# A one-token gated decode kernel: the order of the last weight loads, and the engine that sums w2

## The chip, the cores and the metric

The kernel runs on one core of a Trainium2 chip. Its engines are named as in the profile: TensorE (PE, matrix products; PEld is its weight load), VectorE (DVE), ScalarE (ACT), GpSimd (POOL) and SyncE (SP, which here only issues transfers). The metric is device time in microseconds. Three runs of the kernel before gave 693.84 to 693.93 us, with a median of 693.9 us.

## The reference

One token x (512 values) goes through two branches that a gate mixes. Everything is float32.

```python
x = A_x
g = _sigmoid((x * gate_w).sum(-1, keepdims=True))
a = _A_ref(x, A_k_cache, A_v_cache, A_wq, A_wo)   # attention
b = _B_ref(x, B_w1, B_w3, B_w2)                   # (silu(x w1) * (x w3)) w2
return g * a + (1 - g) * b
```

The attention has 32 query heads and 8 key/value heads of 128, with 32,768 positions in the cache: q = x wq, a softmax over q k / sqrt(128), the weighted sum of v, and then a product of all 4,096 head outputs with wo (4096 x 512). The other branch has 1,792 hidden values, and w2 is 1792 x 512. The key cache and the value cache are 128 MiB each; wo and wq are 8 MiB each, w1, w3 and w2 3.5 MiB each.

## The kernel before

The two caches are read once, each in 16 units of 8 MiB, through two buffers, `big_a` and `big_b`, and a third, `pool_w`, of 4 MiB. All of these loads are issued by SP, in the order in which the program names them; the helper `load` (L190) also makes a load wait until the load nine places earlier has landed, and each load waits until the readers of its buffer are done.

`Program` (L24) is a small scheduler: each operation names what it reads and writes, every engine gets its operations in the order in which the program text names them, and waits are set from these names. So the order of the text is the order of each engine's queue.

The main loop (from L491) goes over the 16 units of keys. A unit is transposed on DVE (L346), multiplied with the query on PE (L330), and every four units the scores are turned and pass a softmax. The units of values follow four steps behind: unit s is half e = s % 2 of head h = s // 2. `values_all` (L426) multiplies it with the weights, and `own` (L442) picks each head's own columns out of the product: a multiply by a mask into `tmp`, and, after a head's second half, a sum over eight blocks into `red[h]`. w1 and w3 come in the middle of the loop, and `hidden` leaves the second branch's hidden values, already times 1 - g, in `htp`: partition p and column k hold hidden value 14 p + k. The last four units of values (12 to 15, heads 6 and 7) come after the loop, and with them all that the change touches:

- `norm` (L533) sums the softmax's denominators over the partitions and takes their reciprocals times the gate.
- `heads` (L541) turns `red[h]` into columns on PE and scales them into `on`: 4 query heads for each key/value head.
- `place` (L553) brings these columns into the layout in which wo's rows lie on the partitions: a multiply on DVE, a product with `spot` on PE, a multiply by a mask on DVE and a sum on DVE.
- `values` (L579) multiplies one half of a unit with the softmax's numerators, 16 products of 128x512, each recorded as two passes.
- `last_head` (L594) does for heads 6 and 7 what `own` and `heads` do for the others, in four operations on DVE, a product and a scaling.
- `mix` (L572) sums 16 rows of wo for each partition on DVE, into `acc`. That is the first half of wo, which waits in `pool_w`; the second half goes through PE.
- `wide` (L656) and `ff_down` (L672) are the last products. `wide` adds products of 32 columns with 128x512 pieces of a weight into the bank `pa`; DVE adds `pa` to `acc`; `ff_down` multiplies the last rows and `acc` (by ones, which sums over the partitions) into the bank `pb`, which is copied out and stored.

The order of the last loads is: unit 12 into `big_a`, the first half of wo into `pool_w`, unit 13 into `big_b`, unit 14 into `big_a`, unit 15 into `big_b` in two halves, the second half of wo and then w2 in five pieces, both into `big_a`. Heads 0 to 5 are laid out (`heads(range(6))` and two calls of `place`) ahead of unit 12's products. Products named `idle_product` (L643) compute nothing that is used.

Of the kernel before, what the change touches and what calls it, by code (L numbers as in the profile page):

```python
# [9 lines left out]
ALU = mybir.AluOpType  # L10
AX = mybir.AxisListType
PE = mybir.EngineType.PE

P = 128
# [102 lines left out]
def kernel(  # L117
# [14 lines left out]
    _, HKV, S, DH = k_cache.shape  # L132
    D = x.shape[-1]
# [27 lines left out]
    def sbuf(name, *shape):  # L161
        return nc.alloc_sbuf_tensor(name, [P, *shape], F32)[:]
# [5 lines left out]
    wo_t = pool_w.rearrange("p (k e) -> p k e", k=16)  # L168
    wo_l = big[0][:, R:2 * R].rearrange("p (k e) -> p k e", k=16)
    sb = sbuf("sb", 16, 32, 4)  # L170
    win = sbuf("win", NP, 4, 48)
# [7 lines left out]
    red = [sbuf(f"red{h}", P) for h in range(6)]  # L179
    acc = sbuf("acc", 512)  # L180
    otp = sbuf("otp", 16, 32)
# [8 lines left out]
    def load(dst, src, writes, over=()):  # L190
        lanes[0] += 1
        lane = f"load{lanes[0] % 9}"
        return pr.add(
            "SP", lambda: nc.sync.dma_start(dst, src), writes=writes, over=[*over, lane], inc=lane, by=16, also=lane,  # L194
        )

    def region(b, z):
        return big[b][:, z * R:(z + 1) * R]
# [8 lines left out]
    own_b, own_q, own_k, own_x = sbuf("own_b", 4), sbuf("own_q", 4), sbuf("own_k", 16), sbuf("own_x", 8)  # L207
    spot, mask, xp = sbuf("spot", 16, 8), sbuf("mask", 16), sbuf("xp", NC, 32)
# [11 lines left out]
    for n, t in (  # L220
        ("win0", win), ("otp", otp), ("mt", mt), ("pvpad", pv[:, 512:528]), ("pad0", prob[0][:, 1024:1040]), ("pad1", prob[1][:, 1024:1040])
    ):
        pool(lambda t=t: G.memset(t, 0.0), writes=[n])

    for src, dst, view, axes in (
        ("ident", "fold", "p (c r) -> p r c", dict(c=4)),
        ("fold", "own_b", "p (b q) -> p b q", dict(b=4)),
        ("fold", "own_q", "p (b q) -> p q b", dict(b=4)),

        ("ident", "own_k", "p (x k) -> p k x", dict(k=16)),  # L230
        ("ident", "own_x", "p (x k) -> p x k", dict(k=16)),
        ("ident", "mask", "p (t x) -> p t x", dict(t=16)),
    ):
        tiles = dict(ident=ident, fold=fold, own_b=own_b, own_q=own_q, own_k=own_k, own_x=own_x, mask=mask)
        s = tiles[src][:, 0:16] if src == "fold" else tiles[src]
        dve(lambda s=s, d=tiles[dst], v=view, a=axes: V.tensor_reduce(d, s.rearrange(v, **a), axis=AX.X, op=ALU.add),
            reads=[src], writes=[dst])
    dve(lambda: V.tensor_copy(spot, own_x.unsqueeze(1).to_broadcast([P, 16, 8])), reads=["own_x"], writes=["spot"])
# [23 lines left out]
    for c in range(NC):  # L262
# [14 lines left out]
    dve(lambda: V.tensor_mul(gpr, rows[0][0:1, :], rows[1][0:1, :]), reads=["row0", "row1"], writes=["tmp1"])  # L277
# [3 lines left out]
    dve(lambda: V.tensor_scalar(gate[:, 1:2], gate[:, 0:1], -1.0, 1.0, op0=ALU.mult, op1=ALU.add),  # L281
        reads=["gate0"], writes=["gate1"])
# [159 lines left out]
    def own(s):  # L442
        h, e = divmod(s, 2)
        dve(lambda: V.tensor_tensor(
            tmp[:, e], ps_o.rearrange("p (b d) -> p b d", b=4), own_b.unsqueeze(2).to_broadcast([P, 4, P]), op=ALU.mult,
        ), reads=["o", "own_b"], writes=[f"tmp{e}"])
        if e == 1:
            dve(lambda: V.tensor_reduce(red[h], tmp.rearrange("p e b d -> p d (e b)"), axis=AX.X, op=ALU.add),  # L448
                reads=["tmp0", "tmp1"], writes=[("red", h)])
# [75 lines left out]
    own_rows = sbuf("own_rows", 16)  # L525
    each = [sbuf(f"each{i}", 16, 8 * n) for i, n in enumerate((2, 1))]


    def load_wo(j, dst, key, over=()):
        load(dst, wo[j * 16 * P:(j + 1) * 16 * P, :].rearrange("(p k) e -> p k e", k=16), [key], over=over)  # L530


# [20 lines left out]
    def place(ws, rows, part, keys, over=()):  # L553
        i, n = 2 - len(ws), 8 * len(ws)
        o, m = 8 * ws[0], 8 * (ws[0] % 2)
        mine = each[i]
        dve(lambda: V.tensor_mul(
            mine, on[:, o:o + n].unsqueeze(1).to_broadcast([P, 16, n]), own_k.unsqueeze(2).to_broadcast([P, 16, n]),
        ), reads=["own_k"] + [("on", 2 * w + u) for w in ws for u in range(2)], writes=[f"each{i}"])
        pe(lambda: T.matmul(  # L560
            pm[i][:, 0:16 * n], spot.rearrange("p t x -> p (t x)"), mine.rearrange("p k t -> p (k t)"),
            start=True, stop=True,
        ), reads=["spot", f"each{i}"], writes=[f"m{i}"])
        dve(lambda: V.tensor_mul(
            mine, pm[i][:, 0:16 * n].rearrange("p (k t) -> p k t", t=n),
            mask[:, m:m + n].unsqueeze(1).to_broadcast([P, 16, n]),
        ), reads=[f"m{i}", "mask"], writes=[f"each{i}"])
        dve(lambda: V.tensor_reduce(rows[part], mine[part], axis=AX.X, op=ALU.add),
            reads=[f"each{i}", *over], writes=keys)


    def mix():  # L572
        for k in range(16):
            dve(lambda k=k: V.scalar_tensor_tensor(
                acc, wo_t[:, k, :], own_rows[:, k:k + 1], acc, op0=ALU.mult, op1=ALU.add,
            ), reads=["wo", "own01", "acc"], writes=["acc"])
# [17 lines left out]
    def last_head(h):  # L594
        r = red[h % 2]
        dve(lambda: V.tensor_scalar(r, ps_o[:, 0:P], own_b[:, 0:1], None, op0=ALU.mult),  # L596
            reads=["o", "own_b"], writes=[("red", h % 2)])
        for b in range(1, 4):
            dve(lambda b=b: V.scalar_tensor_tensor(
                r, ps_o[:, b * P:(b + 1) * P], own_b[:, b:b + 1], r, op0=ALU.mult, op1=ALU.add,  # L600
            ), reads=["o", "own_b", ("red", h % 2)], writes=[("red", h % 2)])
        pe(lambda: T.matmul(pm[1][:, 0:REP], r, own_q, start=True, stop=True), reads=["own_q", ("red", h % 2)], writes=["m1"])
        dve(lambda: V.tensor_mul(on[:, 4 * h:4 * h + 4], pm[1][:, 0:REP], recip[:, 4 * h:4 * h + 4]),
            reads=["m1", ("recip", 3)], writes=[("on", h)])

    def load_unit(b, s):
        load(big[b], vd[s // 2, s % 2], ["AB"[b] + str(z) for z in range(2)])

    full, late = slice(0, P), slice(P // 2, P)
    lay = otp[:, :, 0]  # L610
    load_unit(0, 12)
    load_wo(0, wo_t, "wo", ["kt0"])
    load_unit(1, 13)
    own(11)
    norm(range(4))
    heads(range(6))
    place((0, 1), own_rows, full, ["own01"])
    place((2,), lay, full, ["own2"], ["otp"])
# [11 lines left out]
    load_wo(1, wo_l, "A1")  # L630


    w2t = region(0, 0)[:, 0:FR * D].rearrange("p (k e) -> p k e", k=FR)
    w2d = w2.rearrange("(p k) e -> p k e", k=FR)
# [19 lines left out]
    pa, pb = pf[0], pf[1]  # L654

    def wide(ws, **kw):  # L656
        def go():
            for j, (w, t, first, last) in enumerate(ws):
                r = 32 * (j % 4)
                ins = T.matmul(pa[r:r + 32, :], w, t, start=first, stop=last)  # L660
            return ins
        pe(go, writes=["f0"], **kw)

    wide([(otp[:, k, :], wo_l[:, k, :], k < 4, False) for k in range(16)], reads=["own2", "own3", "otp", "A1"])
    for a, b in parts[:2]:
        wide([(htp[:, k, :], w2t[:, k, :], False, k >= 4) for k in range(a, b)], reads=["htp", ("w2", a)])
# [3 lines left out]
    flat = htp.rearrange("p k a -> p (k a)")  # L670
# [94 lines left out]
```

## Time and profile before

| what | value |
|---|---|
| median of the runs | 693.9 us |
| span of the profiled execution | 692.1 us |
| its own time | not given beside it; the median lies 1.8 us above its span |
| read from memory | 296.23 MB, 428 GB/s over the span |
| busy share of the span | PE 56%, DVE 53%, ACT 19%, POOL 0% |
| mean granted clock of TensorE | 0.802 |

A timeline row gives its start and its duration in microseconds, the engine, the line of the kernel, the operation, what it writes and reads, and how many instructions are merged; in brackets stands the idle time of the engine just before it and what ended it. In a table of stretches, each row gives the busy time of every engine in one stretch, then TensorE's granted clock, the DMA share and GB/s. "us to landing" counts from the issue of a load to the event that its data is there, and holds the time in which it stands in the queue behind earlier loads.

### The profile page before, as it was taken

To read this page: it belongs to the slowest core of one execution; us is meant where nothing else is said; L and a number is where in the kernel's file an instruction comes from. 1 tells how busy PE (TensorE), PEld (TensorE's weight loads), DVE (VectorE), ACT (ScalarE), POOL (GpSimd) and SP (SyncE) were. 2 spreads that over 40 slices of the span, in tenths; PEclk is the share of its full clock that TensorE was granted. 3 is DMA by queue.
4 is the path that set the end of the run, shared out by engine and by line. 5 is a ranking of instruction groups with operands and counts; after the bars stand their busy time and mean duration, and the time that the engine had idled before them with its cause. 6 is when DMAs were issued, how large, how long until landed. Compare 5 with 4: busy or idle time off the path is not lost. (4 is left out here: it accounts for less than half of the span.)

```text
span 692.1 us, 5789 instructions
## 1 busy us (share of the span) xinstructions
PE 388.3 (56%) x2448; PEld 95.3 (14%) x2448; DVE 370.1 (53%) x259; ACT 134.7 (19%) x113; POOL 2.8 (0%) x15
## 2 busy tenths in 40 slices
PE   1537677566473636565564646364563646564457
PEld 0101111201010101201010101101010101211112
DVE  1049998493725637493826537492816547600701
ACT  0143323222303131220303131220303031100000
POOL 1000000000000000000000000000000000000000
PEclk9969999968686966778695779788697879865789
DMA  9999999999999999999999999999999999999996
GB/s 394 444 432 424 428 424 432 449 439 432 424 432 424 443 447 432 428 428 428 432 443 443 428 428 428 428 443 447 432 424 428 428 436 439 421 451 425 422 429 287
DMA packets 6213, 296.35 MB, mean 428 GB/s; under 512 B 694, under 2 KB 698, under 8 KB 1084
## 3 DMA queue, kind: packets, MB, share of 16 engines
q1 hardware_dynamic: 6196, 296.23, 99.1%
q8 instruction: 6, 0.10, 0.1%
q14 instruction: 3, 0.02, 0.0%
q10 hardware_dynamic: 8, 0.01, 0.0%
HBM read 296.23 MB, written 0.00 MB: 428 GB/s over the span
## 5 line engine op out<-in xcount | busy, mean ns | idle before, releaser
L346 DVE STREAM_TRANSPOSE aside<-big_a 128x2048 f32<-128x2048 f32 x41 | 94.4, 2302 | 184.3 <-DMA big_a<-in_A_k_cache_dram 184.3
L330 PE MATMUL ps<-aside,winc 128*32 128x512 f32 x512 | 89.4, 776 | 168.0 <-PEq L703 167.2
L330 PE MATMUL ps<-kt,winc 128*32 128x512 f32 x512 | 89.0, 772 | 49.1 <-PEq L703 49.1
L318 ACT COPY aside<-big_a 128x6144 f32<-128x6144 f32 x14 | 74.4, 5313 | 171.2 <-DMA big_a<-in_A_k_cache_dram 171.2
L432 PE MATMUL ps<-big_b,pv 128*32 128x512 f32 x768 | 94.9, 650 | 17.4 <-PEq L703 17.4
L346 DVE STREAM_TRANSPOSE kt<-aside 128x2048 f32<-128x2048 f32 x32 | 72.7, 2273 | 0.0
L346 DVE STREAM_TRANSPOSE kt<-big_a 128x2048 f32<-128x2048 f32 x28 | 63.5, 2269 | 0.0
L330 PEld LDWEIGHTS ps<-aside,winc 128*32 128x32 f32 x512 | 13.1, 120 | 236.6 <-issue 236.6
L358 ACT COPY sb<-ps 128x512 f32<-128x512 f32 x16 | 17.1, 1071 | 136.5 <-PE ps L330 136.5
L432 PEld LDWEIGHTS ps<-big_b,pv 128*32 128x32 f32 x768 | 27.7, 119 | 85.0 <-issue 85.0
L346 DVE STREAM_TRANSPOSE aside<-aside 128x2048 f32<-128x2048 f32 x16 | 36.3, 2269 | 0.0
L587 PE MATMUL ps<-big_b,probs 128*32 128x512 f32 x128 | 19.1, 756 | 21.1 <-DMA big_b<-in_A_v_cache_dram 21.1
L330 PEld LDWEIGHTS ps<-kt,winc 128*32 128x32 f32 x512 | 13.1, 120 | 125.4 <-issue 125.4
L596 DVE TENSOR_SCALAR red<-ps,own_b 128x128 f32<-128x128 f32 x2 | 0.7, 350 | 52.7 <-PE ps L587 52.7
L324 ACT COPY winc<-win 128x128 f32<-128x128 f32 x32 | 9.8, 307 | 77.9 <-PE ps L330 77.9
L587 PE MATMUL ps<-big_a,probs 128*32 128x512 f32 x128 | 18.1, 730 | 7.6 <-DMA big_a<-in_A_v_cache_dram 7.6
L346 DVE STREAM_TRANSPOSE aside<-big_b 128x2048 f32<-128x2048 f32 x7 | 16.0, 2291 | 11.0 <-DMA big_b<-in_A_k_cache_dram 11.0
L641 PE MATMUL ps<-win,ones 128*128 128x512 f32 (+1 forms) x40 | 21.8, 631 | 0.0
L242 PE MATMUL ps<-acc 128*128 128x512 f32 x34 | 20.0, 670 | 2.5 <-POOL acc L213 1.5
L379 DVE TENSOR_REDUCE mt<-turned 128x8 f32<-128x2048 f32 x4 | 9.2, 2292 | 20.3 <-PE turned L368 20.3
L405 DVE TENSOR_REDUCE sums<-probs 128x8 f32<-128x2048 f32 x4 | 15.3, 3834 | 2.1 <-ACT probs L398 2.1
L268 PE MATMUL turned<-big_a,xp 128*32 128x512 f32 x64 | 8.6, 699 | 12.0 <-DMA big_a<-in_A_wq_dram 12.0
(94 smaller groups left out, 186.9 us busy)
## 6 DMA issues: line engine op xcount, KB each, us to landing
big_b<-in_A_v_cache_dram SPq DMA_DIRECT2D x2, 4096.0 KB, 25.8
big_b<-in_B_w_dram SPq DMA_DIRECT2D x2, 3584.0 KB, 20.8
aside<-in_A_wo_dram SPq DMA_DIRECT2D x1, 4096.0 KB, 29.4
big_a<-in_A_wo_dram SPq DMA_DIRECT2D x1, 4096.0 KB, 20.4
big_a<-in_B_w_dram SPq DMA_DIRECT2D x2, 1024.0 KB, 23.5
big_a<-in_B_w_dram SPq DMA_DIRECT2D x1, 768.0 KB, 26.0
big_a<-in_B_w_dram SPq DMA_DIRECT2D x1, 512.0 KB, 26.7
big_a<-in_B_w_dram SPq DMA_DIRECT2D x1, 256.0 KB, 26.9
```

The costliest lines, as they stand in the source:

```text
L242: return T.matmul(ps_s, acc[:, 0:P], acc, start=True, stop=False, skip_group_check=True)
L268: ins = T.matmul(pf[b][32 * j:32 * j + 32, :], xp[:, c, :], t[:, o:o + REP * DH], start=(c == 0), stop=(c == NC - 1),)
L318: act(lambda: A.copy(spare, src[:, :, 32:128]), reads=[key], writes=["wo"])
L324: lambda: A.copy(winc, win[:, t // 4, :, 16 - 16 * z:48 - 16 * z]),
L330: ins = T.matmul(ps_s[32 * g:32 * g + 32, :], winc[:, c, :], kt[c % 2][:, 512 * g:512 * g + 512], start=False, stop=False, skip_group_chec ...
L346: k = dve(lambda d=dst, s=src: V.transpose(d, s), reads=[key], writes=[f"kt{c % 2}"], credit="keys")
L358: lambda: A.copy(sb[:, :, :, t % 4], ps_s.rearrange("p (n i) -> p n i", i=32)),
L379: dve(lambda: V.tensor_reduce(mt[:, 0:8], turned.rearrange("p (n q) -> p q n", q=8), axis=AX.X, op=ALU.max), reads=banks, writes=["mt"])
L405: dve(lambda: V.tensor_reduce(sums[:, 8 * w:8 * w + 8].rearrange("p (u q) -> p u q", u=2), probs[:, :, 0:1024].rearrange("p u (n q) -> p u ...
L432: ins = T.matmul(ps_o[32 * t:32 * t + 32, :], pv[:, o:o + 32], big[1][:, n * P:(n + 4) * P], start=((z, g) == (0, 0)), stop=((z, g) == (1, ...
L587: ins = T.matmul(ps_o[32 * t:32 * t + 32, :], prob[u][:, o:o + 32], vt[:, n * P:(n + 4) * P], start=((e, z, g) == (0, 0, 0)), stop=((e, z, ...
L641: return T.matmul(bank[:, 0:n], ones, win.rearrange("p w c n -> p (w c n)")[:, 0:n], start=True, stop=True)
```

## The change

It does six things.

1. wo is no longer cut in two. It is loaded whole, last, into `big_a`, with 32 of its rows on each partition (`wo_t`), in six pieces of 16, 7, 3, 3, 2 and 1 rows. `mix` and its load go.
2. w2 goes into `pool_w` in one load, issued behind unit 15, ahead of wo. Its product with `htp` is now 14 operations on DVE that add into `acc`.
3. Unit 15 is one load, not two halves.
4. `place` is called twice, once for each half of the heads, behind head 7; `heads` takes all eight heads at once there. It works on 512 elements of each partition, where it had 256 or 128. `norm` stays where it was.
5. `own_head` takes the place of `last_head`: one multiply of 512 elements and one sum over four blocks. `otp`, now 32 x 32, lies in the buffer `kt1` and is cleared on POOL once the scores are done.
6. The masks of the setup, a multiply for the gate and 1 - g are made on POOL, where DVE made them.

The tail's products change places: `wide` takes the first three pieces of wo (26 rows), `ff_down` the last three (6 rows), with the product with `acc` behind the first of these.

```diff
-    wo_t = pool_w.rearrange("p (k e) -> p k e", k=16)
-    wo_l = big[0][:, R:2 * R].rearrange("p (k e) -> p k e", k=16)
+    wo_t = big[0].rearrange("p (k e) -> p k e", k=32)
+    w2t = pool_w[:, 0:FR * D].rearrange("p (k e) -> p k e", k=FR)
...
-    otp = sbuf("otp", 16, 32)
+    otp = kt[1][:, 0:1024].rearrange("p (k c) -> p k c", c=32)
...
+    def summed(dst, src, key, name, o):
+        half = part4[:, o:o + dst.shape[1] * 2].rearrange("p (r c) -> p r c", c=2)
+        pool(lambda: G.tensor_add(half, src[:, :, 0:2], src[:, :, 2:4]), reads=[key], writes=["half" + name])
+        pool(lambda: G.tensor_add(dst.unsqueeze(2), half[:, :, 0:1], half[:, :, 1:2]), reads=["half" + name], writes=[name])
...
+    summed(fold, ident.rearrange("p (c r) -> p r c", c=4), "ident", "fold", 0)
+    summed(own_b, fold[:, 0:16].rearrange("p (b q) -> p b q", b=4), "fold", "own_b", 64)
+    summed(own_q, fold[:, 0:16].rearrange("p (b q) -> p q b", b=4), "fold", "own_q", 72)
+    banded(own_x, 4, 32, "own_x")
+    banded(mask, 32, 4, "mask")
+    pool(lambda: G.tensor_copy(spot, own_x.unsqueeze(1).to_broadcast([P, 32, 4])), reads=["own_x"], writes=["spot"])
...
-    dve(lambda: V.tensor_mul(gpr, rows[0][0:1, :], rows[1][0:1, :]), reads=["row0", "row1"], writes=["tmp1"])
+    pool(lambda: G.tensor_mul(gpr, rows[0][0:1, :], rows[1][0:1, :]), reads=["row0", "row1"], writes=["tmp1"])
...
+    def place(g):
+        mine, part = each[g], slice(64 * g, 64 * g + 64)
         dve(lambda: V.tensor_mul(
+            mine, on[:, 16 * g:16 * g + 16].unsqueeze(1).to_broadcast([P, 32, 16]), fold.unsqueeze(2).to_broadcast([P, 32, 16]),
+        ), reads=["fold"] + [("on", h) for h in range(4 * g, 4 * g + 4)], writes=[f"each{g}"], over=[("sb", m) for m in range(4)])
         pe(lambda: T.matmul(
+            pm[g], spot.rearrange("p t x -> p (t x)"), mine.rearrange("p k t -> p (k t)"), start=True, stop=True,
+        ), reads=["spot", f"each{g}"], writes=[f"m{g}"])
         dve(lambda: V.tensor_mul(
+            mine[part], pm[g][part].rearrange("p (k t) -> p k t", t=16),
+            mask[part, 16 * g:16 * g + 16].unsqueeze(1).to_broadcast([64, 32, 16]),
+        ), reads=[f"m{g}", "mask"], writes=[f"each{g}"])
+        dve(lambda: V.tensor_reduce(otp[part, :, 0], mine[part], axis=AX.X, op=ALU.add),
+            reads=[f"each{g}", "otp"], writes=[("lay", g)])
...
+    def own_head(h):
+        dve(lambda: V.tensor_tensor(
+            tmp[:, h - 6], ps_o.rearrange("p (b d) -> p b d", b=4), own_b.unsqueeze(2).to_broadcast([P, 4, P]), op=ALU.mult,
+        ), reads=["o", "own_b"], writes=[f"tmp{h - 6}"])
+        dve(lambda: V.tensor_reduce(red[h], tmp[:, h - 6].rearrange("p b d -> p d b"), axis=AX.X, op=ALU.add),
+            reads=[f"tmp{h - 6}"], writes=[("red", h)], over=[("sb", m) for m in range(4)])
...
     load_unit(0, 12)
-    load_wo(0, wo_t, "wo", ["kt0"])
     load_unit(1, 13)
+    pool(lambda: G.memset(otp, 0.0), writes=["otp"], over=["kt1"])
     own(11)
     norm(range(4))
-    heads(range(6))
-    place((0, 1), own_rows, full, ["own01"])
-    place((2,), lay, full, ["own2"], ["otp"])
...
-    last_head(6)
-    for z in range(2):
-        load(region(1, z), vd[7, 1][:, z * R:(z + 1) * R], [f"B{z}"])
-    mix()
+    own_head(6)
+    load_unit(1, 15)
+    load(w2t, w2.rearrange("(p k) e -> p k e", k=FR), ["w2"], over=["wo", "kt0"])
     for z in range(2):
         values(7, 0, z, region(0, z), f"A{z}")
...
-    parts = ((0, 4), (4, 8), (8, 11), (11, 13), (13, 14))
+    wod = wo.rearrange("(p k) e -> p k e", k=32)
+    parts = ((0, 16), (16, 23), (23, 26), (26, 29), (29, 31), (31, 32))
     for a, b in parts:
-        load(w2t[:, a:b, :], w2d[:, a:b, :], [("w2", a)], over=["A0"])
+        load(wo_t[:, a:b, :], wod[:, a:b, :], [("wo", a)], over=["A0", "A1"])
...
-    values(7, 1, 0, region(1, 0), "B0")
-    values(7, 1, 1, region(1, 1), "B1")
-    idle_product(512)
-    last_head(7)
-    idle_product(256)
-    place((3,), lay, late, ["own3"], ["own2"])
+    for z in range(2):
+        values(7, 1, z, region(1, z), f"B{z}")
+    own_head(7)
...
+    heads(range(8))
+    for g in range(2):
+        place(g)
     for _ in range(2):
         idle_product(512)
+    for k in range(FR):
+        dve(lambda k=k: V.scalar_tensor_tensor(
+            acc, w2t[:, k, :], htp[:, k, 0:1], acc, op0=ALU.mult, op1=ALU.add,
+        ), reads=["w2", "htp", "acc"], writes=["acc"])
+    laid = ["otp", ("lay", 0), ("lay", 1)]
+    for i, (a, b) in enumerate(parts[:3]):
+        wide(i, [(otp[:, k, :], wo_t[:, k, :]) for k in range(a, b)], reads=[*laid, ("wo", a)])
     dve(lambda: V.tensor_add(acc, acc, pa), reads=["acc", "f0"], writes=["acc"])
...
-    for a, b in parts[2:]:
-        ff_down([(shifted(k), w2t[:, k, :], k == 8, k == FR - 1) for k in range(a, b)], reads=["htp", ("w2", a)])
-        if a == 8:
+    for a, b in parts[3:]:
+        ff_down([(shifted(k), wo_t[:, k, :], k == 26, k == 31) for k in range(a, b)], reads=[*laid, ("wo", a)])
+        if a == 26:
             ff_down([((ones[:, 0:32],) * 2, acc, False, False)], reads=["ones", "acc"])
```

More of the change, by code (lines that the diff above doesn't have):

```diff
@@ L167 @@
     kt = [pool_w[:, NB * 96:NB * 128], sbuf("kt1", NB * 32)]
-    wo_t = pool_w.rearrange("p (k e) -> p k e", k=16)
-    wo_l = big[0][:, R:2 * R].rearrange("p (k e) -> p k e", k=16)
+    wo_t = big[0].rearrange("p (k e) -> p k e", k=32)
+    w2t = pool_w[:, 0:FR * D].rearrange("p (k e) -> p k e", k=FR)
     sb = sbuf("sb", 16, 32, 4)
+    after = sb.rearrange("p n i m -> p (n i m)")
     win = sbuf("win", NP, 4, 48)
@@ L178 @@
     silu, prod = (tmp[:, i].rearrange("p b d -> p (b d)") for i in range(2))
-    red = [sbuf(f"red{h}", P) for h in range(6)]
+    red = [sbuf(f"red{h}", P) for h in range(6)] + [after[:, P * i:P * i + P] for i in range(2)]
+    each = [after[:, 256 + 512 * i:768 + 512 * i].rearrange("p (k t) -> p k t", t=16) for i in range(2)]
     acc = sbuf("acc", 512)
-    otp = sbuf("otp", 16, 32)
+    otp = kt[1][:, 0:1024].rearrange("p (k c) -> p k c", c=32)
     htp = sbuf("htp", FR, 32)
@@ L206 @@
     ident, ones, fold = sbuf("ident", P), sbuf("ones", P), sbuf("fold", 32)
-    own_b, own_q, own_k, own_x = sbuf("own_b", 4), sbuf("own_q", 4), sbuf("own_k", 16), sbuf("own_x", 8)
-    spot, mask, xp = sbuf("spot", 16, 8), sbuf("mask", 16), sbuf("xp", NC, 32)
+    own_b, own_q, own_x = sbuf("own_b", 4), sbuf("own_q", 4), sbuf("own_x", 4)
+    spot, mask, xp = sbuf("spot", 32, 4), sbuf("mask", 32), sbuf("xp", NC, 32)
     gate, sums, recip, on = sbuf("gate", 2), sbuf("sums", 32), sbuf("recip", 32), sbuf("on", 32)
@@ L220 @@
     for n, t in (
-        ("win0", win), ("otp", otp), ("mt", mt), ("pvpad", pv[:, 512:528]), ("pad0", prob[0][:, 1024:1040]), ("pad1", prob[1][:, 1024:1040])
+        ("win0", win), ("mt", mt), ("pvpad", pv[:, 512:528]), ("pad0", prob[0][:, 1024:1040]), ("pad1", prob[1][:, 1024:1040])
     ):
         pool(lambda t=t: G.memset(t, 0.0), writes=[n])
[L225 to L237, printed above, removed]
@@ L238, with banded @@
-    dve(lambda: V.tensor_copy(spot, own_x.unsqueeze(1).to_broadcast([P, 16, 8])), reads=["own_x"], writes=["spot"])
+    def summed(dst, src, key, name, o):
+        half = part4[:, o:o + dst.shape[1] * 2].rearrange("p (r c) -> p r c", c=2)
+        pool(lambda: G.tensor_add(half, src[:, :, 0:2], src[:, :, 2:4]), reads=[key], writes=["half" + name])
+        pool(lambda: G.tensor_add(dst.unsqueeze(2), half[:, :, 0:1], half[:, :, 1:2]), reads=["half" + name], writes=[name])
+    def banded(dst, n, width, name):
+        shape = [[-width, n]]
+        pool(lambda: G.memset(dst, 1.0), writes=[name + "a"])
+        pool(lambda: G.affine_select(
+            out=dst, in_=dst, compare_op=ALU.is_ge, fill=0.0, base=0, pattern=shape, channel_multiplier=1,
+        ), reads=[name + "a"], writes=[name + "b"])
+        pool(lambda: G.affine_select(
+            out=dst, in_=dst, compare_op=ALU.is_ge, fill=0.0, base=width - 1, pattern=[[width, n]], channel_multiplier=-1,
+        ), reads=[name + "b"], writes=[name])
@@ L280 @@
     act(lambda: A.activation(gate[:, 0:1], pm[0][:, 0:1], AF.Sigmoid), reads=["m0"], writes=["gate0"])
-    dve(lambda: V.tensor_scalar(gate[:, 1:2], gate[:, 0:1], -1.0, 1.0, op0=ALU.mult, op1=ALU.add),
-        reads=["gate0"], writes=["gate1"])
+    pool(lambda: G.tensor_scalar(gate[:, 1:2], gate[:, 0:1], -1.0, 1.0, op0=ALU.mult, op1=ALU.add),
+         reads=["gate0"], writes=["gate1"])
     for b in range(2):
@@ L522 @@
     total(NP - 1)
[L525 to L530, printed above, removed]
     def norm(ws):
@@ L592, in values @@
         pe(go, reads=[key, f"pad{u}", ("prob", u)], writes=["o"])
[L594 to L604, printed above, removed]
+    def own_head(h):
[4 more added lines that the diff above has]
+            reads=[f"tmp{h - 6}"], writes=[("red", h)], over=[("sb", m) for m in range(4)])
     def load_unit(b, s):
         load(big[b], vd[s // 2, s % 2], ["AB"[b] + str(z) for z in range(2)])
-    full, late = slice(0, P), slice(P // 2, P)
-    lay = otp[:, :, 0]
     load_unit(0, 12)
-    load_wo(0, wo_t, "wo", ["kt0"])
     load_unit(1, 13)
+    pool(lambda: G.memset(otp, 0.0), writes=["otp"], over=["kt1"])
     own(11)
     norm(range(4))
-    heads(range(6))
-    place((0, 1), own_rows, full, ["own01"])
-    place((2,), lay, full, ["own2"], ["otp"])
     for z in range(2):
@@ L644, in idle_product, with wide, go @@
         pe(lambda: spend(ps_s, n), reads=["ones"], writes=["s"])
-    values(7, 1, 0, region(1, 0), "B0")
-    values(7, 1, 1, region(1, 1), "B1")
-    idle_product(512)
-    last_head(7)
-    idle_product(256)
-    place((3,), lay, late, ["own3"], ["own2"])
+    for z in range(2):
+        values(7, 1, z, region(1, z), f"B{z}")
+    own_head(7)
+    pa, pb = pf[0], pf[1]
+    wides = [b - a for a, b in parts[:3]]
+    final = {j % 4: (i, j) for i, n in enumerate(wides) for j in range(n)}
+    def wide(i, ws, **kw):
+        def go():
+            for j, (w, t) in enumerate(ws):
+                r = 32 * (j % 4)
+                ins = T.matmul(pa[r:r + 32, :], w, t, start=(i == 0 and j < 4), stop=(final[j % 4] == (i, j)))
+            return ins
+        pe(go, writes=["f0"], **kw)
+    heads(range(8))
+    for g in range(2):
+        place(g)
     for _ in range(2):
         idle_product(512)
[L654 to L666, printed above, removed]
+    for k in range(FR):
[5 more added lines that the diff above has]
+        wide(i, [(otp[:, k, :], wo_t[:, k, :]) for k in range(a, b)], reads=[*laid, ("wo", a)])
     dve(lambda: V.tensor_add(acc, acc, pa), reads=["acc", "f0"], writes=["acc"])
-    flat = htp.rearrange("p k a -> p (k a)")
+    flat = otp.rearrange("p k c -> p (k c)")
     def ff_down(ws, **kw):
```

23 lines of the change are left out of this document (1 added, 22 removed).

## The prediction, on record before the result was known

> **What bounds the kernel now.** I read the page's head and its DMA rows first, then the end of the chain of waits, then the timeline of SP, TensorE (PE) and VectorE (DVE) over the last 100 us.
>
> ```profile
> span 692.1 us, 5789 instructions
> ...
> DMA  9999999999999999999999999999999999999996
> GB/s 394 444 432 424 428 424 432 449 439 432 424 432 424 443 447 432 428 428 428 432 443 443 428 428 428 428 443 447 432 424 428 428 436 439 421 451 425 422 429 287
> ```
>
> The DMA engines are busy in every slice but the last. The kernel is one stream of 296 MB, and its time is the stream's length plus what follows the last landing. The change moves the same bytes, so the question is what hangs behind the last loads.
>
> ```profile
> 661.57 26.71 DMA big_a<-in_B_w_dram
> ...
> 688.32 1.10 PE turned L676 x24
> ...
> 689.44 0.29 DVE winc L688
> ```
>
> Today the last piece of w2 lands, 24 product passes follow, and the copy of the result starts at 689.44. The span ends 2.66 us after that (692.1 - 689.44), and the median of the runs, 693.9, lies 1.8 us above the span. Both stay, so I forecast the start of that copy and add its shift to 693.9.
>
> ```profile
> 617.87 0.33 SPq L194 DMA_DIRECT2D big_a<-in_A_v_cache_dram  x1
> ...
> 631.73 9.75 PE L587 MATMUL ps<-big_b,probs 128*32 128x512 f32 x64 [13.93 <-DMA big_b<-in_A_v_cache_dram]
> ...
> 638.11 3.76 SPq L194 DMA_DIRECT2D big_b<-in_A_v_cache_dram  x2
> ...
> 651.09 8.61 PE L587 MATMUL ps<-big_a,probs 128*32 128x512 f32 x64 [7.59 <-DMA big_a<-in_A_v_cache_dram]
> ...
> 659.77 0.33 SPq L194 DMA_DIRECT2D big_a<-in_A_wo_dram  x1
> ...
> 660.80 3.64 PE L587 MATMUL ps<-big_b,probs 128*32 128x512 f32 x32 [1.11 <-DMA big_b<-in_A_v_cache_dram]
> ...
> 670.51 5.70 PE L587 MATMUL ps<-big_b,probs 128*32 128x512 f32 x32 [6.07 <-DMA big_b<-in_A_v_cache_dram]
> ```
>
> Loads land in the order of their issue, 9.7 us for each 4 MiB (660.80 to 670.51), though issued 10 to 20 us earlier. So a load's landing follows from the bytes ahead of it.
>
> **The loads, moved.** Before, 4 MiB of wo go ahead of the last three v units. After, they go behind. Ahead of the end of the last v unit (unit 15) then lie exactly the bytes that now lie ahead of its first half, so it lands at 660.80 (now 670.51), w2 (3.5 MiB, 8.5 us) at 669.3, the first 16 rows of wo at 679.0, and the last piece where it lands now, about 688.9: its last three pieces have the sizes of today's last three.
>
> Does the stream stay fed? Each v unit's buffer comes free when the products of the unit before last end. With landings 9.7 us earlier: unit 13 lands at 622.0, its products end by 631.8 (9.75), so unit 15 is issued at 631.8, and unit 14 lands at 641.4. That is 9.6 us of cover. wo is issued after unit 14's products, by 651.2, and w2 lands at 669.3. w2 itself stands behind unit 15 in SP's queue, and its buffer is free long before. If a cover of 9.6 us were gone, the price would be the gap. I put the loads at nothing.
>
> **The setup, moved to POOL.**
>
> ```profile
> 3.63 0.16 POOL L223 MEMSET probs<- 128x16 f32 x2
> ...
> 23.01 8.62 PE L268 MATMUL turned<-big_a,xp 128*32 128x512 f32 x64 [12.02 <-DMA big_a<-in_A_wq_dram]
> ...
> 31.56 0.38 PE L279 MATMUL ps<-gsm,ones 1*128 1x1 f32 x2
> ```
>
> POOL's queue is empty at 3.8 us. It gets 14 more small operations in the setup, ahead of the gate's product, whose partner on PE runs at 31.56 behind the products with wq, themselves waiting for a DMA until 23.01. At a whole microsecond each (from the 0.08 us of the row above that is far up) they would end at 18. Cost: nothing, hidden under wq's load. The memset of the new otp waits on POOL for the last score products (about 583) and is wanted first near 677. Nothing again.
>
> **Head 6 and what went before it.** The products of heads 0 to 5 and two placings (601.69 to 608.33 in the trace) leave the path ahead of unit 12's products. That only frees a buffer sooner, under a stream that is never starved: no gain. The 16 products of `mix` on DVE with the first half of wo go too, from a stretch where DVE waits anyway (643.62 to 656.17).
>
> **The chain behind unit 15.** It is new: everything of all eight heads is now laid out here, and the 14 sums with w2 stand behind the layout in DVE's queue.
>
> ```profile
> 593.29 1.12 PE L242 MATMUL ps<-acc 128*128 128x512 f32 x2
> ...
> 599.05 0.68 DVE L444 TENSOR_TENSOR tmp<-ps,own_b 128x512 f32<-128x512 f32 x1
> ...
> 599.76 1.87 DVE L448 TENSOR_REDUCE red<-tmp 128x128 f32<-128x1024 f32 x1
> ...
> 601.69 2.72 PE L546 MATMUL ps<-own_q,red 128*128 128x4 f32 x12 [2.10 <-DVE red L448]
> ...
> 604.44 0.18 DVE L549 TENSOR_TENSOR on<-ps,recip 128x24 f32<-128x24 f32 x1 [2.27 <-PE ps L546]
> ...
> 605.14 1.22 PE L560 MATMUL ps<-each,spot 128*128 128x256 f32 x2 [0.73 <-DVE each L557]
> 606.40 0.42 DVE L564 TENSOR_TENSOR each<-ps,mask 128x256 f32<-128x256 f32 x1 [1.31 <-PE ps L560]
> 606.86 0.42 DVE L568 TENSOR_REDUCE own_rows<-each 128x16 f32<-128x256 f32 x1
> ...
> 607.53 0.80 PE L560 MATMUL ps<-each,spot 128*128 128x128 f32 x2 [1.17 <-DVE each L557]
> ...
> 608.26 9.54 PE L587 MATMUL ps<-big_a,probs 128*32 128x512 f32 x64
> ...
> 643.12 0.39 PE L602 MATMUL ps<-own_q,red 128*128 128x4 f32 x2 [1.64 <-DVE red L599]
> ...
> 643.62 12.55 DVE L574 SCALAR_TENSOR_TENSOR acc<-aside,own_rows,acc 128x512 f32<-128x512 f32 x16
> ```
>
> ```profile
> 676.14 1.13 PE L641 MATMUL ps<-win,ones 128*128 128x512 f32 x2
> ...
> 679.35 0.29 DVE L564 TENSOR_TENSOR each<-ps,mask 128x128 f32<-128x128 f32 x1 [0.58 <-PE ps L560]
> ...
> 686.38 0.69 DVE L667 TENSOR_TENSOR acc<-acc,turned 128x512 f32<-128x512 f32 x1 [6.43 <-PE turned L660]
> 687.10 0.86 PE L676 MATMUL turned<-big_a,htp 128*32 128x128 f32 x24 [0.78 <-DMA big_a<-in_B_w_dram]
> ...
> 687.78 0.40 PE L676 MATMUL turned<-acc,ones 128*32 128x128 f32 x8
> ```
>
> Step by step from 660.80, waits of 0.03 to 0.08 between engines included:
> - Unit 15's 64 product passes in one piece. The samples are 9.54, 9.75, 8.61, and 5.70 + 3.64 for the two halves. I take their mean, 9.3: 670.1.
> - Own columns: multiply 0.68; sum over four, 0.94 (half of the 1.87 for eight), with 0.11 of waits: 671.83.
> - Heads, 16 passes. At half clock 2.72/12 each, 3.6 in all; at full clock one head's two passes take 0.39, of which a second pass adds about 0.13, so about 2.2. With 0.05 ahead: 674.1. The scaling (0.18 and gaps): 674.3.
> - Two placings, one after the other, since the second's first multiply stands behind the first's last sum. Each is a multiply, a 128x512 product, a multiply, a sum, all on 512 elements. 128 elements take 0.29, 256 take 0.42, so 512 take 0.69, as the add of L667 does. The product takes 1.13 at full clock (L641). With 0.16 of waits one placing is 3.36; both end at 681.0.
> - 14 sums with w2, each 12.55/16 = 0.784: 10.98, so 692.0. w2 has been there since 669.3; they wait for nothing but their place in the queue.
> - The add of the bank of wo products, 0.72 with its wait: 692.7. That bank is done well before: 26 rows at 3.64 for 16 from about 682, the last of them landing near 685.5.
> - Behind it in PE's queue stand the product with `acc` (8 passes) and the last three rows of wo (24 passes). Those 32 passes take 1.08 (687.10 to 688.18 today): 693.8. The copy starts at 693.9.
>
> So with TensorE at full clock throughout, the copy starts 4.4 us later than 689.44. wo, landed by 688.9, waits for DVE.
>
> **The clock.** This chain has TensorE working in short bursts, and its granted clock falls after pauses:
>
> ```profile
> 599.00:600.00 1.00, 0.41 (x2) 0.30 (x2) 0.96 (x3) 0.00 (x0) 0.00 (x0) 0.81 0.76 328
> 600.00:601.00 1.00, 0.00 (x0) 0.00 (x0) 1.00 (x1) 0.00 (x0) 0.00 (x0) 0.50 0.77 328
> ...
> 641.00:644.00 3.00, 0.86 (x10) 0.30 (x2) 1.86 (x6) 0.00 (x0) 0.00 (x0) 1.00 1.16 502
> 644.00:645.00 1.00, 0.00 (x0) 0.00 (x0) 0.96 (x2) 0.00 (x0) 0.00 (x0) 0.50 0.61 262
> ```
>
> ```profile
> 602.50:612.00 9.50, 7.60 (x33) 3.82 (x37) 2.23 (x7) 0.00 (x0) 0.00 (x0) 0.50 1.04 448
> ```
>
> The third number from the end is the clock (the last two are the DMA share and GB/s). It fell at about 599.8, 5.4 us after the products that ended at 594.4, and at 644.0, 2.5 us after those that ended at 641.5, in spite of a head's burst at 643.12. So a pause of 2.5 to 5.4 us drops it, short bursts not always helping. After 670.1 the second placing's product comes 8 us after the last dense work, with PE busy about half of that time or less. I take it at half clock. Between 602.5 and 612 the clock was 0.50, and there 128 columns took 0.80 and 256 took 1.22, so 512 would take about 2.08 for 1.13: +0.95; both ends, 0 and 0.95, stay in the range, and so do 0 to 0.95 for the first placing and 0 to 1.4 for the heads (3.6 for 2.2). The last 32 passes come some 4 us after the products with wo have run out; 4 us is about two thirds of the way from 2.5 to 5.4, so I take two thirds of doubling 1.08: +0.7, ends 0 and 1.08. Sum: 4.4 + 0.95 + 0.7 = 6.1 us, and 693.9 + 6.1 = **700.0 us**.
>
> The Trainium skill ("TensorE: Matmul & The Clock Gate", Part 1) states that TensorE goes back to half rate after at least one idle window of about 3.4 us. The trace agrees in kind only: idle stretches of 2.5 and 5.4 us both bracket it. By the rule alone the gaps between the placings (under 2.3 us) cost nothing and the pause before the end costs its 1.08, so the sum would be 5.5 us, 699.4.
>
> **The rivals.**
> - *Full clock all the way*: bursts and the two idle products keep TensorE up. For it: at 643.12 a burst still ran at full clock. Against it: the fall at 644.0. It gives 4.4, with 8.6 instead of 9.3 for unit 15 3.7: 697.6 to 698.3.
> - *Half clock all the way* from the heads: 4.4 + 1.4 + 0.95 + 0.95 + 1.08 = 8.8, or 702.7. For it: at 601.69 the heads ran so, 7 us after the last dense work. Against: here they start 1.7 us after.
> - *The sums are hidden*: the stream still sets the end, about 693.9, or at best some tenths less for fewer small pieces. It decides if the layout is done by 677.2 (688.9 for the last landing, less 10.98 and 0.72), that is if the chain from 660.80 takes 16.4 us and not 20.2. The shortest samples for everything give 19.5, so DVE would have to take the sums between the placings, or the sums would have to take 0.5 us each. w2 is in place at 669.3, which speaks for it; the order of DVE's queue speaks against it.
>
> **How the numbers follow.** The forecast (one placing and part or all of the end at half clock, 5 to 7.5 us) gets 0.5; full clock 0.22; half clock throughout 0.15; hidden sums 0.13. The range leaves out the last and a bit of the third: 697.2 (shortest samples) to 703.0. A measurement here can tell about 0.2%, 1.4 us, from no change. Slower by more takes all but the hidden case: 0.87. Of its 0.13, 0.1 is no change and 0.03 faster.
>
> **What would show it.** In the profile after: unit 15's products start near 660.8 and end near 670; w2 landed before that; 14 operations of 0.78 us back to back on DVE from 681 to 692; TensorE idle for some microseconds ahead of the product with `acc`; the chain of waits ends through DVE and not through a DMA; DMA quiet from 689. I would be wrong if the sums began before 678, if the copy's release were a DMA landing, or if a gap stood in the DMA row before 687.

## The result, and the profile after

The kernel after takes 700.37 us (median of 5 runs, 699.85 to 703.13), the kernel before 693.9 us (median of 5 runs, 693.84 to 694.2). The medians lie 6.5 us apart, 0.9%. The ratio over the runs is 1.0101, with a 95% interval of 1.0089 to 1.0112: slower by about 1%. The five runs after fall into two groups, three at 699.85 to 700.37 and two at 702.22 and 703.13. The profiled execution took 699.88 us with a span of 698.1 us, again 1.8 us apart. Its page:

```profile
span 698.1 us, 5779 instructions
...
DMA  9999999999999999999999999999999999999993
GB/s 410 429 421 424 436 422 457 426 424 447 439 428 428 421 454 436 424 428 432 454 424 428 421 451 439 428 421 428 458 432 421 424 443 451 421 428 424 425 424 149
```

The stream is as full as before up to the last slice, and there it is thinner: 149 GB/s, where before it was 287. The span goes on when the transfers are done. The chain of waits of the kernel after (start, length, what) says through what:

```profile
631.86 29.33 DMA big_b<-in_A_v_cache_dram
...
661.23 8.74 PE ps L579 x64
...
669.99 0.70 DVE tmp L587
670.72 1.05 DVE sb L590
...
671.82 1.96 PE ps L548 x16
...
692.73 0.76 DVE acc L644
...
693.58 0.70 DVE acc L650
...
694.33 1.13 PE turned L659 x32
695.48 0.29 DVE winc L671
```

The last DMA in it is unit 15, landed at 661.2. Before, the last DMA in the chain was the last piece of the stream, a load of w2 that landed at 688.27; now no load that is issued behind unit 15 is in it. The copy starts at 695.48, 6.04 us later than before. The timeline of the same kernel has the middle:

```profile
673.80 0.19 DVE L551 TENSOR_TENSOR on<-ps,recip 128x32 f32<-128x32 f32 x1 [2.04 <-PE ps L548]
674.03 0.69 DVE L557 TENSOR_TENSOR sb<-on,fold 128x512 f32<-128x512 f32 x1
...
674.77 2.07 PE L560 MATMUL ps<-sb,spot 128*128 128x512 f32 x2 [1.01 <-DVE sb L557]
...
678.93 2.07 PE L560 MATMUL ps<-sb,spot 128*128 128x512 f32 x2 [2.09 <-DVE sb L557]
...
682.49 10.99 DVE L644 SCALAR_TENSOR_TENSOR acc<-aside,htp,acc 128x512 f32<-128x512 f32 x14
...
693.58 0.69 DVE L650 TENSOR_TENSOR acc<-acc,turned 128x512 f32<-128x512 f32 x1
```

Both products of the placings took 2.07 us; the granted clock was 0.50 for most of the first and all of the second, where the same size took 1.13 us at full clock before. Then the 14 sums run back to back for 10.99 us. The products with wo started at 684.35, behind the two idle products, which at half clock took 3.62 us:

```profile
680.80 3.62 PE L618 MATMUL ps<-win,ones 128*128 128x512 f32 x4
...
684.35 6.08 PE L634 MATMUL turned<-big_a,kt 128*32 128x512 f32 x49
```

The table of stretches shows the clock (third number from the end) and the stream (the last):

```profile
672.00:676.00 4.00, 2.99 (x18) 2.17 (x17) 0.88 (x2) 0.00 (x0) 0.00 (x0) 0.85 0.95 410
676.00:680.00 4.00, 1.91 (x3) 0.55 (x3) 1.96 (x3) 0.00 (x0) 0.00 (x0) 0.50 0.91 388
680.00:684.00 4.00, 4.00 (x6) 1.29 (x4) 2.85 (x4) 0.00 (x0) 0.00 (x0) 0.50 0.99 411
684.00:686.00 2.00, 2.00 (x17) 0.47 (x20) 1.89 (x4) 0.00 (x0) 0.00 (x0) 0.75 0.98 397
686.00:688.00 2.00, 2.00 (x24) 0.57 (x20) 1.90 (x3) 0.00 (x0) 0.00 (x0) 1.00 0.56 218
688.00:690.00 2.00, 2.00 (x23) 0.62 (x18) 1.93 (x3) 0.00 (x0) 0.00 (x0) 1.00 0.04 14
690.00:692.00 2.00, 1.52 (x31) 0.67 (x22) 1.89 (x4) 0.00 (x0) 0.00 (x0) 1.00 0.00 0
692.00:694.00 2.00, 0.00 (x0) 0.00 (x0) 1.86 (x3) 0.00 (x0) 0.00 (x0) 1.00 0.00 0
```

In the last row only VectorE works: TensorE has nothing to do and the transfers are over.

### The profile page after: what moved, and what is told of

It is laid out like the page before. It is cut to its first block, busy times and chain, and to the rows that moved or that the text cites. A ratio compares the mean times of both kernels' runs of the same rounds, so it can differ in the third digit from the quotient of the medians.

```text
span 698.1 us, 5779 instructions
## 1 busy us (share of the span) xinstructions
PE 386.2 (55%) x2446; PEld 96.1 (14%) x2446; DVE 367.3 (53%) x239; ACT 134.6 (19%) x113; POOL 7.3 (1%) x30
## 5 line engine op out<-in xcount | busy, mean ns | idle before, releaser
L340 PE MATMUL ps<-aside,winc 128*32 128x512 f32 x512 | 86.6, 753 | 169.5 <-PEq L686 168.7
L340 PE MATMUL ps<-kt,winc 128*32 128x512 f32 x512 | 86.4, 751 | 53.1 <-PEq L686 53.1
L587 DVE TENSOR_TENSOR tmp<-ps,own_b 128x512 f32<-128x512 f32 x2 | 1.4, 692 | 63.0 <-PE ps L579 63.0
L618 PE MATMUL ps<-win,ones 128*128 128x512 f32 x36 | 21.7, 693 | 0.0
## 6 DMA issues: line engine op xcount, KB each, us to landing
aside<-in_B_w_dram SPq DMA_DIRECT2D x1, 3584.0 KB, 37.5
```

What stands on the lines that cost most here:

```text
L340: ins = T.matmul(ps_s[32 * g:32 * g + 32, :], winc[:, c, :], kt[c % 2][:, 512 * g:512 * g + 512], start=False, stop=False, skip_group_chec ...
L618: return T.matmul(bank[:, 0:n], ones, win.rearrange("p w c n -> p (w c n)")[:, 0:n], start=True, stop=True)
```

## The experiments

The theory: everything from the landing of unit 15 on is one chain through TensorE and VectorE, and the sums with w2, which stand at its end in VectorE's queue, push it past the stream. The rivals: the late layout or the order of the loads costs the 6 us; the sums are hidden; the setup on POOL costs something.

**The sums taken off VectorE.** Instead of `for k in range(FR): dve(...)`, with w2's rows as a new first piece of `wide` (the lines that change in `wide` itself are left out here):

```diff
+    def hidden_rows(ks):
+        wide(0, [(k, htp[:, k, :], w2t[:, k, :]) for k in ks], reads=["htp", "w2"])
+    hidden_rows(range(0, 8))
     heads(range(8))
+    hidden_rows(range(8, 10))
     place(0)
+    hidden_rows(range(10, 14))
     place(1)
```

> w2's 14 rows are multiplied on TensorE into the same bank as wo's (8 rows ahead of the heads, 2 and 4 ahead of the placings), and VectorE's 14 sums go. Theory (the 11 us of sums behind the layout set the end): the copy of the result falls back to the last landing plus about 0.6 us, 693.9 to 695 us, and the chain of waits ends through a DMA of wo. Rival (the late layout itself, or the order of the loads, costs the 6 us): 698 to 700 us, since the loads and the layout stay where they are.

It took 693.97 us (693.77 to 694.59, 10 runs), ratio to before 0.9997 (0.9988 to 1.0007). All of the loss is gone, with the loads in their new order and the layout nearly as late as in after: it ended at 681.06, in after at 682.46. So neither of these costs the 6 us by itself: it takes the sums' 11 us behind the layout. One point was not met: the chain of this run ends through TensorE and VectorE, not through a DMA.

```profile
681.32 6.17 PE turned L634 x52
687.49 0.02 issue
687.51 0.70 DVE acc L652
...
688.25 1.12 PE turned L661 x32
...
689.40 0.29 DVE winc L673
```

The copy starts at 689.40, where before it started at 689.44: this chain and the stream end at nearly the same time.

**Half of the sums.** `range(FR)` becomes `range(7)` in the sums, so this kernel leaves half of w2's product out.

> Only 7 of the 14 sums with w2 are made; rows 7 to 13 of each partition are left out of the output. Theory: 7 x 0.784 = 5.5 us leave the chain, but the add of the bank of wo products then waits for TensorE, which in the profile after ends the 26 rows at 690.9 because of its clock: the sums end near 688, the add comes at 690.9 and not at 693.6, so 2.7 us are gained, about 697.2 us. If nothing but the sums set the end, 694.4. Rival (the sums are hidden under the stream): no change, 700 us.

696.46 us (695.52 to 699.72, 7 runs), ratio 1.0047 (1.0027 to 1.0068). Four runs lie at 695.52 to 696.46, three at 698.92 to 699.72. In the profile, of a run at 696.46, the sums ended at 687.2, and the add waited, as expected, for the products with wo:

```profile
681.74 5.48 DVE L644 SCALAR_TENSOR_TENSOR acc<-aside,htp,acc 128x512 f32<-128x512 f32 x7
...
683.60 5.96 PE L634 MATMUL turned<-big_a,kt 128*32 128x512 f32 x49
...
690.05 0.69 DVE L650 TENSOR_TENSOR acc<-acc,turned 128x512 f32<-128x512 f32 x1 [2.83 <-PE turned L634]
```

So 5.5 us taken off VectorE bring about 3.9 at the median, and in this profile the next wait in line is TensorE's.

**Sums where VectorE waits.** Two behind the heads' products, two behind each placing's; `add_up(ks)` makes the sums of the rows `ks`:

```diff
-    heads(range(8))
+    heads(range(8), lambda: add_up(range(0, 2)))
     for g in range(2):
-        place(g)
+        place(g, lambda g=g: add_up(range(2 + 2 * g, 4 + 2 * g)))
...
+    add_up(range(6, FR))
```

> Six of the 14 sums are put where VectorE waits for TensorE: two behind the heads' products, two behind each placing's product; eight stay behind the layout. Theory (it is the place in VectorE's queue that costs): 6 x 0.784 = 4.7 us leave the chain; the sums end near 688.8, the add then waits for TensorE's products with wo as in the run with half the sums, so about 697.2 us; with those products at full clock 695.2. Rival (the sums' length, wherever they are, or w2's landing): 700 us.

696.8 us (695.48 to 699.65, 6 runs), ratio 1.0047 (1.0028 to 1.0067). No run lies near this median: three are at 695.48 to 695.74, near the 695.2 expected with the products at full clock, and three at 697.86 to 699.65, above the 697.2 expected otherwise. All six are below after's fastest, 699.85. No sum was made cheaper or left out; six only moved in the queue. It is the place of the sums in VectorE's order that costs.

**Idle products around the placings.**

```diff
+    idle_product(512)
     heads(range(8))
-    for g in range(2):
-        place(g)
+    idle_product(256)
+    place(0)
+    idle_product(512)
+    idle_product(256)
+    place(1)
```

> Idle products are put ahead of the heads (512 columns), ahead of the first placing (256) and ahead of the second (512 and 256), in pauses of TensorE that are longer than they are. Theory (both placings ran at half clock): their products take 1.13 us and not 2.07, so the end comes 1.9 us earlier, about 698 us, and the runs spread less than the 699.85 to 703.13 of after. Rival (the 2.07 us belong to the product here, whatever the clock): 700 us or a bit more.

699.65 us (699.46 to 699.95, 4 runs). The spread is as narrow as expected, the gain is not what was expected: 0.7 us at the median instead of 1.9. The timeline shows where it went:

```profile
674.69 1.82 PE L560 MATMUL ps<-sb,spot 128*128 128x512 f32 x2 [0.47 <-DVE sb L557]
...
678.64 1.09 PE L560 MATMUL ps<-sb,spot 128*128 128x512 f32 x2
...
693.05 0.66 PE L663 MATMUL turned<-acc,ones 128*32 128x128 f32 x8 [4.81 <-DVE acc L654]
...
693.48 1.51 PE L663 MATMUL turned<-big_a,kt 128*32 128x128 f32 x24
```

The placings gained 0.25 and 0.98 us. But now the products with wo also ended earlier, TensorE stood idle for 4.81 us ahead of the product with `acc`, its clock fell, and the last 32 passes took 1.98 us, where in after they took 1.13. What was won in the middle was largely given back at the end.

**The pause at the end filled too.** To the kernel just shown, four idle products ahead of the product with `acc`.

```diff
         if a == 26:
+            for _ in range(4):
+                idle_product(512)
             ff_down([((ones[:, 0:32],) * 2, acc, False, False)], reads=["ones", "acc"])
```

> The kernel with idle products around the placings, and four more idle products (512 columns each, about 3.8 us) in the pause of TensorE ahead of the product with acc. In that kernel's profile the clock fell 4 us into this pause and the last 32 passes took 1.98 us. Theory (the pause drops the clock and that eats the gain of the placings): the passes take 1.1 us, the end comes 0.9 us earlier, 698.6 us, and the runs lie close together. Rival (these passes take that long for another reason): 699.6 us.

698.87 us (698.56 to 700.75, 4 runs; three of them within 698.56 to 698.87). The passes took 1.08 us again, and the time fell by 0.8 us. One run lay at 700.75, so the spread was not removed here.

**Unit 15 in two halves.** `load_unit(1, 15)` becomes the two loads of the kernel before.

> Unit 15 in two halves again, as before the change; all else as after. Theory (everything from the landing of unit 15 on is one chain): the first half's products run while the second half lands, so its products end at about 666.3 and not 670.0; the chain moves by the same 3.0 to 3.7 us and the time is about 697 us. Rival (the wait for the sums is set by w2's landing at 669.7, or the end by TensorE's products with wo): less than 1 us, 699 to 700 us.

697.45 us (696.18 to 698.92, 4 runs), ratio 1.0051 (1.0036 to 1.0066): 2.9 us less than after at the median.

```profile
661.11 5.74 PE L579 MATMUL ps<-big_b,probs 128*32 128x512 f32 x32 [6.07 <-DMA big_b<-in_A_v_cache_dram]
...
678.95 10.99 DVE L645 SCALAR_TENSOR_TENSOR acc<-aside,htp,acc 128x512 f32<-128x512 f32 x14
...
690.79 0.65 PE L660 MATMUL turned<-acc,ones 128*32 128x128 f32 x8 [2.53 <-DVE acc L651]
```

The products of unit 15 ended at 666.85 and not at 669.92, and the sums began at 678.95, not at 682.49. They did not wait for w2, which had landed at 669.6. So the sums moved by 3.5 us and the copy by 2.7 us (692.79 for 695.48): the last 32 passes were at half clock here, 1.94 us, after a pause of 2.53 us.

**The setup back on VectorE.** The masks as `tensor_reduce` on VectorE, and the two small operations of the gate.

> The setup's masks, the multiply for the gate and 1 - g go back to VectorE; all else as after. Theory (the setup is hidden under the load of wq): no change against after, 699.9 to 700.4 us, the products with wq start at the same 23 us. Rival (POOL's longer setup, 3 us in the first slice, holds up the start): 0.5 to 3 us faster than after.

699.79 us (699.63 to 702.04, 4 runs), at the lower end of after's runs (699.85 to 703.13), with profiled runs of 699.91 and 699.88; the products with wq started at 22.94 and in after at 23.05. No cost of the setup shows beyond some tenths.

**w2 on TensorE and unit 15 in halves.** The first experiment with two loads for unit 15, without the two idle products behind the placings, and with w2's rows after the heads (2), after the first placing (6) and after the second (6).

> w2 on TensorE as in the first experiment, with unit 15 in two halves, and without the two idle products behind the placings: the layout then stands some 3 us ahead of need. Theory (with the chain off the path the stream sets the end, and its last landing is where it was): 693.7 to 694.0 us, no difference from before, and the chain of waits ends through a DMA. Rival (the late layout still costs some tenths in the first experiment, so that removing it beats the kernel before): 692.5 to 693.3 us.

693.99 us (693.74 to 694.4, 11 runs), ratio 0.9996 (0.9987 to 1.0005): no difference from before. The chain now ends through the last load of wo:

```profile
653.09 35.43 DMA big_a<-in_A_wo_dram
688.52 0.04 issue
688.56 1.08 PE turned L660 x24
...
689.67 0.29 DVE winc L672
```

The layout ended here at 677.84, and TensorE then waited for wo (1.15, 0.56 and 0.82 us). So a tail with time to spare does not beat the kernel before. The stream sets the floor, and no version tried here is clearly below it.

**Sums between, with the clock held up.** The third experiment with four sums in the waits (two, one, one) and the idle products around the placings.

> Four of the sums in VectorE's waits (two behind the heads' products, one behind each placing's) and the idle products around the placings, both edits together. Theory (the spread of the runs with sums between, 695.5 to 699.7 us, is TensorE's clock): with the clock held up the products with wo end at about 687.2 and the sums at 688.5, so 694.8 us with a spread under 1 us. Rival (the spread comes from the loads or from VectorE): again several microseconds of spread.

695.58 us (695.25 to 696.35, 10 runs), ratio 1.0023 (1.0014 to 1.0033). The sums ended at 689.24 and not at 688.5, because unit 15's products took 9.67 us in this profile; that is most of the 0.8 us by which the time missed. The ten runs lie within 1.1 us, where those of the third experiment lay within 4.2.

**Two further runs of the sums between, one of after.** No edit.

> The kernel with six sums in VectorE's waits once more, unchanged, one look: where a run of it lies above 697 us, theory (the clock) expects the landing of unit 15 and the lengths of VectorE's operations as before, and a granted clock of 0.50 through more of the heads, the placings and the products with wo; rival (the loads): a later landing of unit 15 or of wo.

> The same kernel and the same question, a further look, since its runs lie in two groups, near 695.6 and 698 to 699.7 us.

> The kernel after once more, unchanged, one look. Its runs lay at 699.9 and at 702 to 703 us. Theory: a run at 699.9 shows one or both placings at half clock and the last 32 passes at full clock; a run at 702 or more shows half clock from the heads to the end; unit 15 lands at 660.7 to 661.3 in both.

The two runs of the sums between took 697.63 and 695.63 us, with spans of 695.4 and 693.9. Of the first:

```profile
661.21 8.64 PE L581 MATMUL ps<-big_b,probs 128*32 128x512 f32 x64 [9.54 <-DMA big_b<-in_A_v_cache_dram]
...
674.71 2.08 PE L561 MATMUL ps<-sb,spot 128*128 128x512 f32 x2 [1.01 <-DVE sb L558]
...
680.74 3.62 PE L620 MATMUL ps<-win,ones 128*128 128x512 f32 x4
...
690.84 0.69 DVE L655 TENSOR_TENSOR acc<-acc,turned 128x512 f32<-128x512 f32 x1 [2.14 <-PE turned L636]
```

Of the second:

```profile
660.80 9.16 PE L581 MATMUL ps<-big_b,probs 128*32 128x512 f32 x64 [10.71 <-DMA big_b<-in_A_v_cache_dram]
...
674.82 1.64 PE L561 MATMUL ps<-sb,spot 128*128 128x512 f32 x2 [1.01 <-DVE sb L558]
...
680.41 2.73 PE L620 MATMUL ps<-win,ones 128*128 128x512 f32 x4
...
689.34 0.69 DVE L655 TENSOR_TENSOR acc<-acc,turned 128x512 f32<-128x512 f32 x1 [0.98 <-PE turned L636]
```

Unit 15's products began 0.41 us later in the first, but in both they ended within 0.11 us of each other (669.85 and 669.96). The add came 1.50 us later in the first. The placing's product is 0.44 us longer there, and the idle products with which TensorE stands in the way of the products with wo are 0.89 us longer: the clock fell earlier and came back later. Together that is 1.33 of the 1.5 us between the spans; the other 0.5 us between the times lies outside the span. This accounts for a run at 697.63; no run at 698 to 699.7 was profiled, so that the clock makes those too is not shown. The further run of after took 700.62 us. It showed what was expected of a run at 699.9: both placings at 2.08 us, the last passes at full clock, the copy at 694.88. Its time lies 3.0 us above its span of 697.6, where the profiled run of after had 1.8. No profile of a run at 702 or more was caught; those two runs have spans of 700.5 and 700.7, so their 2.5 us are inside the kernel, and what they are stays open. The narrow spreads with idle products speak for the clock, the one run at 700.75 in the fifth experiment speaks against it.

## Why the prediction was right

Forecast were 700.0 us and a shift of the copy by 6.05 us; measured were 700.37 us and a shift of 6.04 us. The mechanism is the one forecast, and the experiments show it: without the sums on VectorE the loss is gone (693.97), and with six of them moved ahead in the queue about half of it is gone at the median (696.8). That the sum agrees to some hundredths is luck: its terms were off by up to 0.94 us, and these errors cancel. The sum fits the profiled run, at 699.88; it has no term for the two runs at 702 and 703. Its terms:

| step | forecast, us | in the profile after, us |
|---|---|---|
| unit 15's products can start | at 660.80 | at 661.23 |
| its 64 passes | 9.3 | 8.69 |
| own columns, sum over four | 0.94 | 1.04 |
| heads, 16 passes | 2.2 | 1.96 |
| placing products | 1.13 and 2.08 | 2.07 and 2.07 |
| 14 sums | 10.98 | 10.99 |
| last 32 passes | 1.08 + 0.7 | 1.13 |
| start of the copy | 695.5 | 695.48 |

- The loads cost nothing, as argued: unit 15 landed within 0.5 us of the place worked out from the bytes ahead of it, w2 before it was wanted, and the stream had no gap.
- The clock was placed wrong in detail. I gave half clock to the second placing and two thirds of it to the end. Both placings had it and the end did not. The two thirds were also misread: 4 us lies about halfway between 2.5 and 5.4, which by the same working gives 0.54 for 0.7 and 699.8 us for the sum. TensorE's pause ahead of the product with `acc` was 2.81 us, not 4. The products with wo ended at 690.86 and not near 688, because they began at 684.35 and not near 682, behind two idle products that took 3.62 us at half clock (1.88 at full clock in before).
- "That bank is done well before" was the weakest sentence. It was done 2.7 us before the add. With half the sums, or with six of them moved, this bank is what the add waits for, so a change that only shortens VectorE's part gets back 3.6 to 3.9 us at the median (the runs spread over 4.2 us) and not the 4.7 to 5.5 of its sums.
- The cost at nothing for the setup was right (699.79 with the setup back on VectorE). Unit 15 in one piece stood in the chain with all its 64 passes; by the sixth experiment some 3 of the 6.5 us go when it is loaded in halves (2.9 at the median, four runs over 2.7 us). This part and the sums' share don't add up to the 6.5, since without the sums the stream covers the later end of unit 15.

On the clock: it fell at about 674.8 in after, 4.9 us after the dense products had ended at 669.9 and in spite of the heads' burst. It fell at about 692 in the fourth experiment, 3.8 us into a pause, and it did not fall within the 2.81 us of after's pause. The Trainium skill ("TensorE: Matmul & The Clock Gate", Part 1) puts the fall after at least one idle window of about 3.4 us. These last two pauses agree with that. The sixth experiment does not: the granted clock was 0.65 between 689 and 690 and 0.50 from there on, so it fell about 1 us into the pause of 2.53 us, 2.7 us after the products with wo of L635 had ended at 686.57, with 24 short passes in between. The placings do not agree either with the reading that I made of it: none of their gaps was longer than 2.1 us, and both ran at half clock. The prediction's "idle stretches of 2.5 and 5.4 us" were no idle stretches: each holds a burst (at 643.12 and at 599.18), and TensorE's longest idle time in them was 1.64 and 4.77 us. How much work within a pause keeps the clock up stays open here.

The rival that the sums are hidden fell. Full clock all the way was not seen in either profile of after, nor was half clock all the way. The lower end of the range, 697.2, lies 0.4 us below the 697.6 that the prediction's own shortest samples give.

## What to carry to other kernels

When a kernel is one full stream of loads, put the last loads in the order in which their work can still be done beneath the stream, and add up the whole chain behind each load, engine by engine, against the time of the last landing. A load that comes early is worth nothing if its work stands behind a late one in an engine's queue: here w2 lay ready at 669.7 (issued at 632.23, landed 37.5 us later) and waited for VectorE until 682.5. When a chain has been shortened, look for the next wait on it and for the clock of a TensorE that now pauses.

## What the runs showed of the hardware that was not expected

- Keeping TensorE busy in one pause can move a pause to another place: idle products around the placings left 4.81 us of idle time at the end, and 0.85 us of the gain was lost there.
- Bursts did not hold the clock. After 669.9 TensorE was busy for 2 us with the heads' products, and the first placing still ran at half clock (2.07 us for 1.13).
- The time of a run lies 1.7 to 3.0 us above its span, and this changes from run to run of the same kernel (1.8 and 3.0 for after).
- A sum over four strided blocks took 1.04 us, a sum over eight 1.87 to 1.93: halving the work saved a bit less than half.
- An operation on 64 partitions took as long as one on 128: 0.68 against 0.69 us for 512 elements.
